# Threshold attention and SoLU: weights converted in 8 rounds, first slots turned by TensorE, slots in the order of token tiles

## The chip, the cores and the metric

The kernel runs on one core of one Trainium2 chip. The metric is the device time in microseconds of one execution. Times of runs are given with the number of runs; times of single instructions come from one profiled execution.

## What is computed

```
scores = (q @ k.T) / 8                       # batch 8, heads 8, sequence 576, head 64
thresh = max(scores, axis=-1) - tau
scores = where(scores >= thresh, scores, -1e9)
attn   = softmax(scores);   y = attn @ v     # -> x: 4608 tokens x 512
h      = x @ w_in                            # 512 x 1024
solu   = h * softmax(h)
ln     = (solu - mean) / sqrt(var + 1e-6) * g_ln
out    = ln @ w_out                          # 1024 x 512
```

All of q, k, v are 32-bit floats. `w_in` and `w_out` come as 64-bit floats[...]: the kernel reads them as integers and builds 32-bit floats from exponent, mantissa and sign.

## The kernel before

The work is cut into 144 *slots* (the list `slots`, L361), 18 for each batch: a slot is 128 queries against the 576 keys of two heads (a pair of heads, `hp`). Kind 0 and 1 are the first and second 256 queries, each in two slots (`r`) for each pair; kind 2 is the last 64 queries. Two slots of one key make a *unit*.

The schedule is written out by hand: the loop at L735 goes round by round, and round `rnd` issues, engine by engine and in this order, what is due. The main items for slot `rnd` are:

- PE: `scores` (L370), preceded by the turning of later q and k blocks (`turn`, L258) into spare columns of the same PSUM tile;
- DVE: `maxes` (L402), a maximum with its negation; ACT: `ramp` (L417, the threshold) and `exps` (L424), with `keeps` that copy turned blocks to SBUF;
- one round later POOL: `normalise` (L432: sum, power -1, two products of 128x576) and DVE: `blocks` (L442: two 32x32 transposes into `T`; after a unit's second slot, four DMAs on SP make `wT` of `T`);
- three rounds after a unit's second slot PE: `attend` (L465, 36 matmuls), and ACT: `attended` (L492).

A token tile (128 tokens) is ready for the feed-forward part (FFN) when the attention of all four pairs of its queries is done. One FFN step at most goes into a round: `h` in two quarters (`ff_h`, L520), then, some rounds later, `o` in two quarters (`ff_o`, L635). Between them DVE, ACT and POOL make the maximum, exponential, norm and the transposition. `preps` (L688) and `load_at` (L699) give the rounds in which later batches' q, k, v are turned and loaded. SP issues nearly all DMAs, in program order.

Tile pools give one buffer for each of the PSUM tags `s0` and `s1` (scores) and `p0` and `p1` (everything else, handed out by `take`, L100): whoever takes a tag waits until its last reader is done.

The weights come in 16 pieces of 128x512 (`piece`, L189): 8 of `w_in`, 8 of `w_out`. Piece x is converted in round x: `weight_a` (L208) cuts out exponent (DVE, then ACT) and mantissa (DVE); `weight_b` (L227) has three DVE operations (low word, sign, product); `weight_d` (L247) makes two SBUF-to-SBUF DMAs for a piece of `w_out`. Loads are three pieces ahead (`weight_load`, L200).

The first batch's q and k are turned by `whole_pair` (L349), which takes both PSUM tags; pairs 1, 2, 3 in rounds 0, 2, 4 (L723), after that round's exponentials.

Of the kernel before, what the change touches and what calls it, by code (L numbers as in the profile page):

```python
# [20 lines left out]
def kernel(  # L21
# [118 lines left out]
    def load_v(b, hf):  # L140
# [3 lines left out]

        d["v"] = loads.tile([P, 4, NK, D], F32, tag="v", bufs=3, name="v")
        rest = v[b, hs, 0:SM, :].rearrange("h (p t) d -> p h (t d)", t=4)
        for to, rows, of in (
            (0, slice(0, P), slice(0, P)), (4, ROWS[0], ROWS[1]), (4, ROWS[1], ROWS[0])
        ):
            nc.sync.dma_start(  # L150
                out=d["v"][rows, :, to : to + 4].rearrange("p h t d -> p h (t d)"), in_=rest[of]
            )
        for rows in ROWS:
            nc.sync.dma_start(
                out=d["v"][rows, :, NK - 1], in_=v[b, hs, SM:S, :].rearrange("h p d -> p h d")
            )
# [41 lines left out]
    raws = {}  # L198

    def weight_load(x):  # L200
        raw = work.tile(
            [P, 512], I64 if wide else F32, tag=("xh2", "xh3", "uT")[x % 3], bufs=1, name="raw"
        )
        queue = nc.scalar if x < 3 else nc.sync
        queue.dma_start(out=raw, in_=piece(x)[0])
        raws[x] = dict(raw=raw)

    def weight_a(x):  # L208
        if not wide:
            return  # L210
        d = raws[x]
        hi = d["raw"].bitcast(I32).rearrange("p (n two) -> p n two", two=2)[:, :, 1]
        d["em"] = e, m = [
            work.tile([P, 512], I32, tag=t, bufs=n, name="em") for t, n in (("ob", 2), ("xe", 1))
        ]
# [4 lines left out]

        nc.scalar.activation(out=e, in_=e, func=AF.Relu, bias=lim, scale=8388608.0)
# [4 lines left out]

    def weight_b(x):  # L227
        d = raws.pop(x)
        _, dst, unit = piece(x)
        if not wide:  # L230
            nc.vector.tensor_scalar(out=dst, in0=d["raw"], scalar1=unit, scalar2=None, op0=ALU.mult)
            return
        words = d["raw"].bitcast(I32).rearrange("p (n two) -> p n two", two=2)
        lo, hi = words[:, :, 0], words[:, :, 1]
        e, m = d["em"]
# [3 lines left out]
        nc.vector.scalar_tensor_tensor(  # L239
            out=e, in0=hi, scalar=-(2**31), in1=e, op0=ALU.bitwise_and, op1=ALU.bitwise_or  # L240
        )
        nc.vector.scalar_tensor_tensor(
            out=dst, in0=dst, scalar=unit, in1=e.bitcast(F32), op0=ALU.mult, op1=ALU.mult
        )


    def weight_d(x):  # L247
        c = x - 2 * NP
# [58 lines left out]

    def k_parts(i):
# [3 lines left out]
    def k_item(i, ts=slice(0, 4)):  # L312
# [8 lines left out]
        def keep(spare, x, r):  # L321
            (nc.vector.tensor_copy if r and not spare.get("eased") else nc.scalar.copy)(
# [6 lines left out]
    def e_item(i):  # L329
# [6 lines left out]
        def keep(spare, x, r):  # L336
# [4 lines left out]
            else:  # L341
                (nc.scalar.copy if spare.get("eased") else nc.vector.tensor_copy)(
                    out=last, in_=seen(spare, 1, x, 1)[:, 0].rearrange("p (k c) -> p c k", c=2)
                )
# [15 lines left out]

    slots = []  # L361
    for b in range(B):
# [3 lines left out]
        slots += [(b, 2, 0, 0), (b, 2, 0, 1)]  # L366

    live = {}

    def scores(s, items):  # L370
# [10 lines left out]
        for ks in (slice(SM, S), slice(0, SM)):  # L381
            for h in range(2):
                for y in range(2):
                    if kind < 2:
                        d = pairs[b * NP + hp]
                        t = P * (2 * kind + r) + 64 * y
                        lhsT = d["qT"][ROWS[h], t : t + 64]
                    else:
                        d = pairs[b * NP + r + 2 * y]
                        lhsT = d["qe"][ROWS[h]]  # L390
                    nc.tensor.matmul(  # L391
                        out=ps[h][ROWS[y], ks], lhsT=lhsT, rhs=d["kT"][ROWS[h], ks],
# [31 lines left out]
    def exps(s):  # L424
        d = live[s]
        d["sm"] = sm = small.tile([P, 2], F32, tag="sm", name="sm")
        for x, w in enumerate(d["w"]):
            nc.scalar.activation(  # L428
# [13 lines left out]
    def blocks(s):  # L442
        b, kind, hp, r = slots[s]
        key = (b, kind, hp)
# [19 lines left out]

    def attend(key):  # L465
        b, kind, hp = key
# [6 lines left out]
        for e in range(2) if kind == 2 else [None]:  # L473
            for m in range(NK):
                for u in range(2):
                    d, h0 = source(b * NP + (hp if e is None else e + 2 * u))
# [15 lines left out]
    def attended(key):  # L492
        b, kind, hp = key
# [8 lines left out]
        else:  # L502
            if hp == 0:
# [3 lines left out]
            to = xh[b, kind][:, hp].rearrange("p (r u y) -> p u r y", r=2, u=2)  # L507
# [168 lines left out]
    PER = NS // B  # L676
# [3 lines left out]
    for s, (b, kind, hp, r) in enumerate(slots):  # L680
        if r == 1:
            pv_due.append((s + LAG_PV + (s < 4), (b, kind, hp)))

    def first_slot(i):
        return PER * (i // NP) + 2 * (i % NP)

# [13 lines left out]
    for b in range(1, B):  # L700
        r = PER * (b - 1)

        for at, job, hf in zip(
            (2, 8, 9) if b > 1 else (8, 12, 15), (load_qk, load_qk, load_v), (0, 1, 0)
# [4 lines left out]
    with tc.manual_schedule():  # L709
        load_qk(0, 0)  # L710
        nc.scalar.dma_start(out=tau_t, in_=tau.partition_broadcast(P))
        constants()
        for x in range(3):
            weight_load(x)
        load_qk(0, 1)
        load_v(0, 0)
        nc.sync.dma_start(out=g_rows, in_=g_ln.rearrange("(c p) -> c p", p=P))
        whole_pair(0)
# [3 lines left out]
        pieces = {r: x for x, r in enumerate(range(16))}  # L722
        whole = {0: 1, 2: 2, 4: 3}  # L723
        load_at[3] = [lambda: load_v(0, 1)]
# [10 lines left out]
        while True:  # L735
# [29 lines left out]
            if more:  # L765
# [7 lines left out]
                scores(rnd, items)  # L773
                maxes(rnd)
                ramp(rnd, 0)
                keeps(rnd, 0)
                keeps(rnd, 1)
                ramp(rnd, 1)
                exps(rnd)
            if rnd in whole:  # L780
                whole_pair(whole[rnd])
            if rnd - 1 in live:
                normalise(rnd - 1)
# [106 lines left out]
```

## Time and profile before

| | |
|---|---|
| runs (3), us | 923.97, 929.83, 930.18; median 929.83 |
| profiled execution, us | 926.31 (span 924.5) |
| granted PE clock, mean | 0.968 |
| PE busy | 854.7 us (92%) |
| PE weight loads | 624.7 us (68%) |
| DVE busy | 679.0 us (73%) |
| ACT busy | 592.0 us (64%) |
| POOL busy | 452.8 us (49%) |
| DMA | 154.6 MB, mean 167 GB/s |
| first maximum (L408) of slots 0, 10, 20, 79, us | 14.8, 69.6, 140.2, 476.1 |

How to read it: the page cuts the span into 40 equal slices of 23.1 us and gives each engine's busy share of a slice in tenths. [...]PE's busy time says that it had work, not that it was at its peak; the length of a step is better read from the starts of successive steps in the timeline. A 32-bit matmul shows as two records. Idle time of an engine that doesn't set the end costs nothing.

### The profile page before, as it was taken

What the parts mean: (1) busy time and instruction counts of PE and PEld (TensorE: products, weight loads), DVE (VectorE), ACT (ScalarE), POOL (GpSimd) and SP (SyncE); (2) the same over time, 40 slices, a digit from 0 to 9 for tenths busy, and PEclk for the clock granted to TensorE, in tenths of its full rate; (3) what the DMA queues carried; (4) which work ended last, traced back from release to release, by engine and by line L of the source; (5) the groups of instructions that cost most, each with busy time, mean ns of one, the idle gap of its engine ahead of it and who ended that gap; (6) DMA issues with size and microseconds to landing.
All of it is one profiled execution on the core that took longest, in us unless ns stands there. A gap on an engine that the chain in (4) does not pass through costs nothing. (4 is left out here: it accounts for less than half of the span.)

```text
span 924.5 us, 39657 instructions
## 1 busy us (share of the span) xinstructions
PE 854.7 (92%) x17089; PEld 624.7 (68%) x17089; DVE 679.0 (73%) x1306; ACT 592.0 (64%) x1240; POOL 452.8 (49%) x870
## 2 busy tenths in 40 slices
PE   4657779989999999989997999999999999999997
PEld 2435457868778778867785667866677777676555
DVE  4998967768867877767876777767877777877352
ACT  4766656767767766767766676757766676776121
POOL 1554545536555555555554555545555455655120
PEclk9788799999999999999999999999999999999999
DMA  8899858985879567965889467965889565766322
GB/s 244 200 260 261 186 124 198 229 179 124 187 169 224 128 140 185 237 150 134 184 183 209 94 136 182 229 150 130 186 185 224 121 131 128 191 145 140 90 47 47
DMA packets 95470, 154.61 MB, mean 167 GB/s; under 512 B 27192, under 2 KB 69184, under 8 KB 95296
## 3 DMA queue, kind: packets, MB, share of 16 engines
q1 hardware_dynamic: 93920, 150.12, 70.3%
q8 instruction: 134, 2.20, 1.1%
q10 hardware_dynamic: 1376, 1.97, 0.6%
q14 instruction: 40, 0.33, 0.1%
HBM read 46.14 MB, written 9.44 MB: 60 GB/s over the span
## 5 line engine op out<-in xcount | busy, mean ns | idle before, releaser
L408 DVE CUSTOM_DVE_ANT_0 w<-s_ps,tau_t 128x576 f32<-128x576 f32 x288 | 206.6, 755 | 157.2 <-PE s_ps L391 133.8
L419 ACT ACTIVATE w<-s_ps,nth 128x576 f32<-128x576 f32 x288 | 207.6, 744 | 127.1 <-DVE nth L408 106.2
L642 PE MATMUL o_ps<-w,uT 64*64 64x256 f32 x4608 | 271.2, 380 | 11.3 <-DVE uT L630 9.0
L642 PEld LDWEIGHTS o_ps<-w,uT 64*64 64x64 f32 x4608 | 221.6, 134 | 70.6 <-issue 27.9
L438 POOL TENSOR_SCALAR w<-w,sm 128x576 f32<-128x576 f32 x288 | 218.6, 771 | 14.3
L428 ACT ACTIVATE w<-w,ntau 128x576 f32<-128x576 f32 x288 | 220.3, 772 | 0.0
L540 PE MATMUL h_ps<-w,xh 64*64 64x512 f32 x1856 | 218.0, 591 | 0.7 <-issue 0.7
L450 DVE STREAM_TRANSPOSE T<-w 128x576 f32<-128x576 f32 x288 | 205.8, 751 | 4.5 <-POOL w L438 4.2
L486 PEld LDWEIGHTS pv<-wT,v 64*64 64x64 f32 x5760 | 168.0, 137 | 44.1 <-issue 24.7
L391 PE MATMUL s_ps<-kT,qT 64*64 64x64 f32 (+1 forms) x2048 | 173.2, 425 | 22.5 <-ACT w L419 19.0
L486 PE MATMUL pv<-wT,v 64*64 64x128 f32 (+1 forms) x5760 | 171.2, 265 | 10.8 <-DMA wT<-T 8.3
L540 PEld LDWEIGHTS h_ps<-w,xh 64*64 64x64 f32 x1856 | 110.1, 134 | 93.3 <-issue 67.9
L435 POOL TENSOR_SCALAR sm<-sm 128x2 f32<-128x2 f32 x144 | 36.1, 251 | 275.7 <-ACT w L428 272.9
L436 POOL TENSOR_TENSOR sm<-sm,mone 128x2 f32<-128x2 f32 x144 | 107.2, 745 | 12.0
L391 PEld LDWEIGHTS s_ps<-kT,qT 64*64 64x64 f32 x2048 | 64.1, 139 | 34.9 <-ACT w L419 24.9
L604 ACT ACTIVATE V<-u,nb,rs 128x1024 f32<-128x1024 f32 x36 | 44.7, 1241 | 53.2 <-POOL nb L594 53.2
L508 ACT COPY xh<-pv 128x256 f32<-128x256 f32 x64 | 23.9, 374 | 68.1 <-PE pv L486 68.1
L630 DVE STREAM_TRANSPOSE uT<-V 128x1024 f32<-128x1024 f32 x36 | 44.1, 1224 | 23.9 <-DMA V<-u 23.9
L562 ACT ACTIVATE u<-h_ps,hm 128x1024 f32<-128x1024 f32 x36 | 40.3, 1118 | 26.4 <-DVE hm L553 20.8
L428 ACT ACTIVATION_READ_ACCUMULATOR w<-w,ntau 128x1 f32 x288 | 57.0, 198 | 0.0
L553 DVE TENSOR_REDUCE hm<-h_ps 128x1 f32<-128x1024 f32 x36 | 43.0, 1195 | 9.4 <-PE h_ps L530 6.0
L568 DVE TENSOR_TENSOR u<-h_ps,u 128x1024 f32<-128x1024 f32 x36 | 42.8, 1189 | 9.6 <-ACT u L562 9.6
(74 smaller groups left out, 609.9 us busy)
## 6 DMA issues: line engine op xcount, KB each, us to landing
wT<-T SPq DMA_DIRECT2D x288, 288.0 KB, 5.7
V<-u SPq DMA_DIRECT2D x144, 64.0 KB, 3.8
out_dram<-ob SPq DMA_DIRECT2D x72, 128.0 KB, 2.8
v<-in_v_dram SPq DMA_DIRECT2D x16, 512.0 KB, 8.3
v<-in_v_dram SPq DMA_DIRECT2D x32, 256.0 KB, 7.6
q<-in_q_dram SPq DMA_DIRECT2D x15, 512.0 KB, 6.1
k<-in_k_dram SPq DMA_DIRECT2D x15, 512.0 KB, 7.2
raw<-in_moe_w_out_dram SPq DMA_DIRECT2D x8, 512.0 KB, 9.2
```

Of the source, the lines that this page charges most:

```text
L391: nc.tensor.matmul(out=ps[h][ROWS[y], ks], lhsT=lhsT, rhs=d["kT"][ROWS[h], ks], start=True, stop=True,)
L408: nc.vector.tensor_tensor_reduce(out=w, in0=ps[:, 0:S], in1=tau_t.to_broadcast([P, S]), scale=1.0, scalar=BIG, op0=ALU.add, op1=ALU.min, a ...
L419: nc.scalar.activation(out=d["w"][x], in_=d["ps"][x][:, 0:S], func=AF.Prelu, bias=d["nth"][x], scale=-1.0, alpha=1.0e30,)
L428: nc.scalar.activation(out=w, in_=w, func=AF.Exp, bias=ntau, scale=1.0, accum_out=sm[:, x : x + 1])
L436: nc.gpsimd.tensor_tensor(out=sm, in0=sm, in1=mone, op=ALU.pow)
L438: nc.gpsimd.tensor_scalar(out=w, in0=w, scalar1=sm[:, x : x + 1], scalar2=1.0, op0=ALU.mult, op1=ALU.mult)
L450: nc.vector.transpose(out=T[:, :, r, h, :], in_=w)
L486: nc.tensor.matmul(out=to, lhsT=d["v"][ROWS[u], h0 + h, m ^ 4 * u if m < 8 else m], rhs=rhs, start=m == 0, stop=m == NK - 1,)
L540: mm = nc.tensor.matmul(out=h[ROWS[y], f], lhsT=x[ROWS[r], c, ROWS[y]], rhs=w1_parts[ROWS[r], c, part ^ r], start=part == 0 and c == 0, st ...
L604: nc.scalar.activation(out=V, in_=u, func=AF.Identity, bias=nb, scale=rs)
L630: nc.vector.transpose(out=uT, in_=d["V"].rearrange("p y (m x) -> p m y x", x=32))
L642: nc.tensor.matmul(out=d["o"][ROWS[z], 512 * r : 512 * r + 256], lhsT=d["uT"][ROWS[r], m].rearrange("p y x -> p (y x)"), rhs=w2[ROWS[r], m ...
```

## The change

- **Weights, two pieces a round in rounds 0 to 7.** `weight_a` takes over the low word's operation (3 on DVE), `weight_b` is ACT's one operation, `weight_c` the sign (DVE), and the product moves to POOL, in two operations (`weight_d`). Loads are five pieces ahead, in other buffers; the first two are issued on ACT's queue before the constants.
- **Slots 0 to 7 turned by PE.** No products, no transposes and no DMAs `wT<-T` for them: POOL makes a diagonal matrix of each head's reciprocal sums (`weigh`), PE multiplies each 128x128 block of the exponentials by it (`early_turn`, 10 matmuls a slot), which turns and normalises at once; DVE and, after round 3, ACT copy the result to SBUF; PE attends one slot at a time (`early_attend`, 10 matmuls), two rounds after the slot. The turned blocks and results use the spare columns of the score tiles and a `p` tag. The first batch's keys are kept in plain order for it (`k_plain`), and POOL copies them to the usual order (`k_spread`).
- **Order of slots.** For kind 0 and 1 of batches 0 and 1 the four pairs of one `r` come first, then those of the other: a token tile is complete after 4 slots instead of 8. A unit of these is two pairs of one `r`, attended in two halves (72 matmuls of 64 columns for 36 of 128).
- **Order of the rest.** `whole_pair` in rounds 0, 1, 2, before the exponentials; the second halves of v's first loads in rounds 6 and 7; batch 1's q, k, v loads at 8, 11, 14 (before: 8, 12, 15); in the first 36 rounds an `attend` may share a round with an `o` step.

The core of the diff:

```diff
+    RAWS = ("xh2", "xh3", "uT", "u", "xh1")
...
+    def scratch():
+        ahead["two"] = two = work.tile([P, 2, DFF // 2], F32, tag="V", bufs=1, name="two")
+        ahead["kT"] = work.tile([P, NP, S], F32, tag="T", name="kT")
+        ahead["ends"] = two[:, 0].rearrange("p (h d) -> p h d", h=H)
+        nc.gpsimd.memset(two[:, 0], 0.0)
+    def load_ends():
+        for e in range(2):
+            nc.sync.dma_start(
...
     def weight_a(x):
...
         nc.vector.tensor_scalar(
             out=e, in0=hi, scalar1=20, scalar2=0x7FF,
             op0=ALU.logical_shift_right, op1=ALU.bitwise_and,
         )
...
         nc.vector.tensor_scalar(
             out=m, in0=hi, scalar1=0xFFFFF, scalar2=0x100000,
             op0=ALU.bitwise_and, op1=ALU.bitwise_or,
         )
...
         nc.vector.scalar_tensor_tensor(
             out=dst, in0=lo.bitcast(U32), scalar=2.0**-32, in1=m, op0=ALU.mult, op1=ALU.add
         )
-        nc.vector.scalar_tensor_tensor(
-            out=e, in0=hi, scalar=-(2**31), in1=e, op0=ALU.bitwise_and, op1=ALU.bitwise_or
-        )
-        nc.vector.scalar_tensor_tensor(
-            out=dst, in0=dst, scalar=unit, in1=e.bitcast(F32), op0=ALU.mult, op1=ALU.mult
-        )
+    def weight_b(x):
+        if wide:
+            e = raws[x]["e"]
+            nc.scalar.activation(out=e, in_=e, func=AF.Relu, bias=lim, scale=8388608.0)
+    def weight_c(x):
+        if wide:
+            e = raws[x]["e"]
+            nc.vector.scalar_tensor_tensor(
+                out=e, in0=words(x)[1], scalar=-(2**31), in1=e,
+                op0=ALU.bitwise_and, op1=ALU.bitwise_or,
+            )
+        if x + len(RAWS) < NW:
+            weight_load(x + len(RAWS), nc.sync)
     def weight_d(x):
...
+            nc.gpsimd.tensor_scalar(
+                out=dst, in0=dst, scalar1=unit, scalar2=1.0, op0=ALU.mult, op1=ALU.mult
+            )
+            nc.gpsimd.tensor_tensor(out=dst, in0=dst, in1=d["e"].bitcast(F32), op=ALU.mult)
...
+    def k_spread(i):
+        of = k_plain(i)
+        to = k_parts(i)
+        first = of[:, 0:SM].rearrange("p (t r k c) -> p r c t k", t=4, r=2, c=2)
+        for r in range(2):
+            nc.gpsimd.tensor_copy(
+                out=to[:, 4 * r : 4 * r + 4].rearrange("p t c k -> p c t k"), in_=first[:, r]
+            )
+        nc.gpsimd.tensor_copy(
+            out=to[:, NK - 1], in_=of[:, SM:S].rearrange("p (k c) -> p c k", c=2)
+        )
...
+    EARLY = 2 * NP
+    OUTER = {(0, 0), (0, 1), (1, 0), (1, 1)}
+    for b, kind in OUTER:
+        o = PER * b + EARLY * kind
+        slots[o : o + EARLY] = [(b, kind, hp, r) for r in range(2) for hp in range(NP)]
...
+    def weigh(s):
+        d = live[s]
+        sm = d["sm"]
+        nc.gpsimd.tensor_scalar(out=sm, in0=sm, scalar1=1e-9, scalar2=None, op0=ALU.add)
+        nc.gpsimd.tensor_tensor(out=sm, in0=sm, in1=mone, op=ALU.pow)
+        d["diag"] = diag = work.tile([P, 2, P], F32, tag="ob", name="diag")
+        for h in range(2):
+            nc.gpsimd.tensor_scalar(
+                out=diag[:, h], in0=ident, scalar1=sm[:, h : h + 1], scalar2=1.0,
+                op0=ALU.mult, op1=ALU.mult,
+            )
+    def early_turn(s, rnd):
+        d = live.pop(s)
+        tag, tp = take("tw")
+        last = live[rnd]["ps"][1][:, S : S + P]
+        for h in range(2):
+            w = d["w"][h]
+            for t in range(5):
+                if t < 4:
+                    o = 512 * h + P * t
+                    to, of = tp[:, o : o + P], w[:, P * t : P * t + P]
+                else:
+                    to, of = last[ROWS[h]], w[:, SM:S]
+                nc.tensor.matmul(out=to, lhsT=of, rhs=d["diag"][:, h], start=True, stop=True)
...
+        on_act = rnd > 3
+        nc.vector.tensor_copy(out=wT[:, 0:4], in_=tp[:, 0:512].rearrange("p (t k) -> p t k", t=4))
+        (nc.scalar.copy if on_act else nc.vector.tensor_copy)(
+            out=wT[:, 4:8], in_=tp[:, 512:1024].rearrange("p (t k) -> p t k", t=4)
+        )
+        (nc.scalar.copy if on_act else nc.vector.tensor_copy)(out=wT[:, 8], in_=last)
+        pairs_free.append(tag)
+    def early_attend(s, rnd):
+        b, kind, hp, r = slots[s]
+        wT = early.pop(s)
+        y = live[rnd]["ps"][0][:, S : S + P]
+        d, h0 = source(hp)
+        for t in range(5):
+            for h in range(2):
+                of = d["v"][:, h0 + h, t] if t < 4 else ahead["ends"][:, 2 * hp + h]
+                nc.tensor.matmul(
+                    out=y[ROWS[h]], lhsT=of, rhs=wT[:, 4 * h + t if t < 4 else 8],
+                    start=t == 0, stop=t == 4,
+                )
...
@@ the loop
+                if rnd - 2 in early:
+                    early_attend(rnd - 2, rnd)
                 maxes(rnd)
+                if rnd < EARLY:
+                    weight_b(2 * rnd)
                 ramp(rnd, 0)
                 keeps(rnd, 0)
                 keeps(rnd, 1)
                 ramp(rnd, 1)
+                early_attended()
+                if rnd < EARLY:
+                    weight_c(2 * rnd)
+                    weight_a(2 * rnd + 1)
+                if rnd in whole:
+                    whole_pair(whole[rnd])
                 exps(rnd)
-            if rnd in whole:
-                whole_pair(whole[rnd])
             if rnd - 1 in live:
-                normalise(rnd - 1)
+                (weigh if rnd - 1 < EARLY else normalise)(rnd - 1)
+            if 0 <= rnd - 1 < EARLY:
+                early_turn(rnd - 1, rnd)
+            if rnd < NP:
+                k_spread(rnd)
...
-            if rnd in pieces:
-                x = pieces[rnd]
-                weight_b(x)
-                if x + 3 < len(pieces):
-                    weight_load(x + 3)
-                if x + 1 < len(pieces):
-                    weight_a(x + 1)
-            if rnd - 1 in pieces:
-                weight_d(pieces[rnd - 1])
-                w2_done = pieces[rnd - 1] == NW - 1
+            if rnd < EARLY:
+                if rnd:
+                    weight_d(2 * rnd - 1)
+                weight_c(2 * rnd + 1)
+                if 2 * rnd + 2 < NW:
+                    weight_a(2 * rnd + 2)
+                weight_d(2 * rnd)
+            elif rnd == EARLY:
+                weight_d(NW - 1)
+                w2_done = True
```

Between the two exponentials of a slot before 8, `exps` also issues `weight_b(2 * s + 1)`.

## The prediction

> **What bounds it now.** I read the page's slices first, then busy time by stretch, then the order of instructions engine by engine, then the timeline of the start. A *round* r is one slot: it runs from the first maximum (L408) of slot r to that of slot r+1.
>
> ```profile
> PE   4657779989999999989997999999999999999997
> DVE  4998967768867877767876777767877777877352
> PEclk9788799999999999999999999999999999999999
> ```
> PE is the bound, except in the first six or seven slices (some 150 us), where DVE is full and PE is not. The stretches say how much:
> ```profile
> core 0: us, PE busy (x) PEld busy (x) DVE busy (x) ACT busy (x) POOL busy (x), PEclk, DMA share, GB/s
> 20.00:40.00 20.00, 11.81 (x209) 7.20 (x209) 19.34 (x41) 16.44 (x37) 10.83 (x15) 0.76 0.71 177
> 60.00:80.00 20.00, 12.69 (x242) 9.74 (x242) 16.08 (x34) 11.27 (x24) 9.45 (x13) 0.76 1.06 270
> 300.00:320.00 20.00, 20.00 (x422) 16.37 (x418) 16.92 (x34) 15.86 (x34) 9.78 (x21) 1.00 0.55 123
> ```
> From 20 to 40 us DVE works 19.3 of 20 us and PE 11.8, at 0.76 of its clock. At 300 us PE works 20.0 of 20.
> PE's timeline where it is full gives the price of a step, start to start:
> ```profile
> 147.16 3.70 PE L540 MATMUL h_ps<-w,xh 64*64 64x512 f32 x32
> 150.59 1.24 PE L391 MATMUL s_ps<-kT,qT 64*64 64x64 f32 x16
> 151.56 3.72 PE L642 MATMUL o_ps<-w,uT 64*64 64x256 f32 x64
> ```
> An `h` step is 3.43, scores about 0.95, an `o` step 3.45 (155.02 to 151.56, the next row); likewise `pv` is 1.96 (164.44 to 166.40), 2.1 when cut in halves, a group of 20 turns 0.6. Rounds summed from these agree with their measured length within 0.2 us wherever PE is full, so I use them for both kernels.
> The last view is POOL beside DVE in the start:
> ```profile
> 62.58 0.75 DVE L242 SCALAR_TENSOR_TENSOR w<-w,gs,em 128x512 f32<-128x512 f32 x1
> 63.25 0.42 DVE L216 TENSOR_SCALAR em<-raw 128x512 int32<-128x512 int32 x1
> 63.58 0.42 DVE L222 TENSOR_SCALAR em<-raw 128x512 int32<-128x512 int32 x1
> ...
> 62.76 1.28 POOL L436 TENSOR_TENSOR sm<-sm,mone 128x2 f32<-128x2 f32 x1
> ...
> 303.77 0.71 POOL L436 TENSOR_TENSOR sm<-sm,mone 128x2 f32<-128x2 f32 x1
> ```
> The same two-element power takes 0.71 us alone and 1.28 beside a weight conversion, ending 0.04 us after DVE's L222 does: POOL is held while DVE converts.
>
> [...] The full-width row (L530) shows 190 ns a load, hidden under 452 ns a matmul (21.7/48).
>
> **Part 1: where the work goes.** The order of PE's instructions has five more FFN steps done by round 20 (12 against 7). But the lead shrinks: steps need attention's results, at most one goes in a round, and the new kernel comes to rounds with none (14, 23, 24, 37, 46, 56, 65, 74). From round 79 both orders are the same, to the last instruction. So the tail isn't shorter; the change is worth what it saves of PE's idle time before round 79, which starts at 476.1 us now. Two stretches follow.
>
> **Part 2: rounds 0 to 9.** Before: 14.8 to 69.6 us, about 5.5 us a round, DVE's sum: maxima 1.35, transposes 1.43, conversion 0.34+0.33+0.60+0.72+0.61=2.6.
> After, per round until 7: DVE 2 conversions of (0.34+0.33+0.60+0.70)=3.94, maxima 1.35, transposes gone; PSUM copies of `wT` instead, 0.62 for 512 columns (by the slope of the `kT` copies, 216 ns at 64 and 416 at 256), 0.22 for 128: all three on DVE in rounds 1 to 3 (6.75 us a round), one from round 4 (5.9). POOL: the two 771 ns products go; it gets two diagonals (0.5), and per weight a scaling (735x512/576=0.65)[...], the sums and powers 1.1, `k_spread` 0.8 in rounds 0 to 3. ACT: 4.5, keeps 1.53 in 0 to 2, copies 0.74 from 4. PE: 10 turning matmuls, 20 records. Unshown; from L530 a quarter of 452, so 20x0.113=2.3 us with loads hidden, 20x(0.113+0.19)=6.1 with none; I take 2.3/0.76=3.0. Early attention 10 matmuls, 1.1 to 2.3; I take 1.4.
> Chains, from the program's waits. In rounds 1 and 2 the turning matmul waits for `whole_pair`'s keeps (same PSUM tag), and the next scores for the third copy (same PSUM tile): first ramp 0.8 after the maximum, two ramps 1.4, keeps 1.5, turning 3.0, copies left 0.85, conversion 2.0: 9.6, in round 2 10.2 with early attention ahead. Round 0, without turning: 7.2. Rounds 3 to 5: DVE's and POOL's conversion work one after the other is 3.94+5.3=9.2 (9.7 in round 3 with parts of it idle-covered); without contention the chain over ACT's copies is 6.3. I take 8.5, 7.8, 7.8. Rounds 6 and 7 hold `h` behind turning: 0.3+1.4+3.0+3.44+0.75=8.9; in 7 also the FFN maximum 1.2 and a conversion step ahead of the next maximum: 10.0. Round 8 6.3 (ACT's chain), round 9 4.5. Sum 80.8. The first maximum stands behind the first conversion, which waits for its weights (L216 at 14.1); they are issued 1.8 us earlier (2.9 against 4.7): start about 13.8. Round 10 is then at 94.6, against 69.6.
> Behind these waits: on PE, the next scores stand behind the turning matmul, and DVE's maxima wait for those; on POOL, `weigh` stands behind two products, and the turning matmul waits for it; on ACT, from round 4 the copies stand behind both exponentials.
> DMAs: 16 `wT<-T` transfers go (4 units, 288 KB each); the weights' 8.4 MB come in 8 longer rounds, below the 246 GB/s that 40 to 60 us shows. Five buffers give a load two rounds (over 14 us) against 9.2 us to landing: nothing, but 1 us of DVE per us late if a load takes longer. On SP, batch 1's q and k (round 8) now queue behind `w2` swaps that wait for POOL; due at round 10, 10.8 us later, landing 6 to 7: nothing, with little to spare; each us later would be a us of round 10.
> Edits at nothing: the second halves of v go from the start to rounds 6 and 7, first used by `pv` in round 13; the two loads of v's ends (POOL zeroes their tile first) are due in round 2, over 15 us after issue; plain keys change the keeps' target only, not their count; the loads at 11 and 14 for 12 and 15 follow the pairs' earlier first slots. Rounds of more than 6 us hide each; bare, each is one landing, 6 to 8 us.
>
> **Part 3: rounds 10 to 78.** PE's work after: 69x0.91 scores + 30x3.44 `h` + 30x3.43 `o` + 17x1.95 + 16x2.10 `pv` + 596x0.03 turns = 353.8. (Before: 360.5, in 406.5 us.) Loss: in before, rounds 20 to 78 lose 19.2 us; 7.1 of it in three rounds with no FFN step (28, 29, 38: 7.6, 4.6 and 4.5 us between their L408 in DVE's timeline, 5.6 on average, for 3.3, 3.5 and 2.9 of PE's work), 0.22 a round elsewhere. After: 61x0.22=13.2, and eight such rounds 8x5.6-25.0=19.6. Sum 386.6. Round 79 then starts at 481.2, 5.1 later than now.
> The profiled execution takes 926.3, so 931.4; on the median 929.8, 934.9. The profiled one lies inside the three runs; I say **934**.
>
> **Rivals.** A chance for each; 1% (9.3 us) is about what a measurement of this kernel can tell from no change.
> *As summed*, 0.42: extra early work eats the saving; -4 to +10, so 926 to 940.
> *Turning matmuls with bare weight loads*, 0.27, slower: a full-width load (190 ns) isn't covered by a 113 ns matmul. At 6.1 instead of 3.0, +3.1 in rounds 1, 2, 6, 7, about 1 in 3: +13.4, 947. It decides from 4.0 us a slot. For it: loads twice as wide as any in the start[...]; against: L530's loads do hide.
> *POOL becomes the bound of rounds 1 to 7*, 0.15: its product takes 2.0 instead of 1.2 held by DVE: 1.6 more in five rounds, +8, 942. For it: the held power; against: POOL is idle half of the time now.
> *The saving stays*, 0.16: rounds without FFN work cost no more than PE's other rounds, the loss falls from 33 to 13 us: 914, and 919 with a little of it. For it: rounds 29 and 38 took 4.5; against: 28 took 7.6.
> *The tail gets shorter by the five steps (17 us)*: excluded by the order from round 79 on.
>
> **The numbers.** Faster 0.15 (the fourth case). Slower: 0.27+0.10 of the third+0.04 of the first=0.41. The rest, 0.44, within 1%. Range 917 to 952: the fourth case's upper part up to the second's, with its clock some 5 us worse.
>
> **What would show it.** Round 10's first maximum near 95 us (before: 69.6); round 79's near 481; turning records of about 150 ns start to start (300 would be the second case); POOL's products over 1.2 us and stretched beside conversions; eight rounds of over 5 us without FFN work. Wrong if round 10 comes before 85 us, or if rounds 10 to 78 take under 370 or over 400.

## The result, and the profile after

The changed kernel takes 987.37 us (median of 4 runs, 985.72 to 1003.04) against 926.9 of the kernel before beside it: 1.0651 times as long, with an interval of 1.0577 to 1.0725. The run of 1003.04 was in a slower state and has no part in the ratio. The profiled execution takes 988.3 (span 986.5). The forecast of 934, with a range up to 952, was wrong by 53 us; "slower" had 0.41.

The slices of the page after, to be laid beside those of before:

```profile
PE   4777878958999989999898999999999999999997
DVE  5774655644677866877686787777777777887442
PEclk9888989978999999999999999999999999999999
```
DVE is no longer full in the first slices (7, 7, 4, 6 in slices 2 to 5 for 9, 9, 8, 9), yet PE isn't either; PE has a 5 in slice 9 (197 to 222 us), and between slices 10 and 22 four digits of 8. The same stretches as before:

```profile
core 0: us, PE busy (x) PEld busy (x) DVE busy (x) ACT busy (x) POOL busy (x), PEclk, DMA share, GB/s
20.00:40.00 20.00, 12.79 (x148) 9.94 (x148) 13.71 (x22) 11.13 (x28) 13.24 (x22) 0.77 0.49 163
60.00:80.00 20.00, 14.69 (x112) 9.48 (x116) 13.48 (x28) 10.36 (x22) 9.15 (x12) 0.83 0.50 129
300.00:320.00 20.00, 17.57 (x494) 12.82 (x489) 13.93 (x27) 12.45 (x29) 9.33 (x19) 1.00 0.79 197
```
From 20 to 40 us DVE works 13.7 of 20 us where it worked 19.3, POOL more (13.2 for 10.8), and no engine is full: a chain of waits from engine to engine sets the rounds. At 300 us PE works 17.6 of 20 at a full clock, although nothing of the new start is left there.

The first maxima (L408 before, L486 after) give the time by stage:

| us | before | predicted | after | after less predicted |
|---|---|---|---|---|
| first maximum | 14.8 | 13.8 | 11.6 | -2.2 |
| rounds 0 to 9 | 54.8 | 80.8 | 101.5 | +20.7 |
| rounds 10 to 78 | 406.5 | 386.6 | 435.1 | +48.5 |
| round 79 to the end of the span | 448.4 | 448.4 | 438.3 | -10.1 |

The differences sum to 56.9, which is 988.3 less the 931.4 that was forecast for the profiled execution.

**Rounds 0 to 9.** Three things stand in the timeline. First POOL's product beside DVE (start, duration, engine and line; the bracket is the idle time before an instruction and what ended it):

```profile
29.81 1.32 POOL L286 TENSOR_TENSOR w<-w,w 128x512 f32<-128x512 f32 x1 [0.69 <-DVE w L271]
29.92 1.49 DVE L253 TENSOR_SCALAR w<-raw 128x512 int32<-128x512 int32 x1
```
L253 takes 0.42 us alone. The product starts when DVE's L271 ends, and here it meets L253, which waits it out: 29.81+1.32 is 31.13, and 29.92+1.49 is 31.41, less than 0.3 us later. It happens to 8 of the 16 pieces, twice in rounds 1 and 2 and once in rounds 0, 3, 4 and 5, and each time L253 takes 1.07 us more.

Second, PE's clock. In rounds 3, 4 and 5 the trace grants half the clock from 51.2 to 54.6, from 61.4 to 64.8 and from 71.6 to 75.0. In these stretches lie the scores and the early attention, for which the next maximum waits. Round 4 of the changed kernel, and after it round 4 of e7 (a run below), where the same rows have the full clock:

```profile
61.22 2.06 PE L469 MATMUL s_ps<-kT,qT 64*64 64x64 f32 x12 [1.62 <-ACT wT L578]
63.21 1.85 PE L589 MATMUL s_ps<-wT,v 128*64 128x128 f32 x16
```
```profile
60.48 1.19 PE L468 MATMUL s_ps<-kT,qT 64*64 64x64 f32 x12 [0.94 <-ACT wT L577]
61.60 1.09 PE L588 MATMUL s_ps<-wT,v 128*64 128x128 f32 x16
```
From the start of these twelve score records to the next maximum it is 4.1 us in each of rounds 3, 4 and 5, and 2.5 at the full clock (rounds 3 to 5 of e3, 4 and 5 of e7): 1.6 us a round.

Third, round 7, from 85.5 to 101.2:

```profile
79.58 3.66 PE L687 MATMUL h_ps<-w,xh 64*64 64x512 f32 x32
83.34 0.10 POOL L106 MEMSET mark<- 128x1 f32 x1 [10.50 <-PE h_ps L687]
...
86.20 1.26 POOL L286 TENSOR_TENSOR w<-w 128x512 f32<-128x512 f32 x1
...
89.03 1.06 POOL L551 TENSOR_SCALAR diag<-ident,sm 128x128 f32<-128x128 f32 x2
89.80 2.08 PE L569 MATMUL tw<-diag,w 128*128 128x128 f32 x8 [4.34 <-POOL diag L551]
```
POOL's queue holds a marker (L106, `fence`, called by `ff_h`) that waits for the first `h` step. POOL stands 10.5 us before it; the conversions of round 6 and the diagonals of round 7 stand behind it, and PE waits 4.3 us for those.

**Rounds 10 to 78.** PE's timeline shows attention in halves stopping in its middle:

```profile
131.47 1.80 PE L629 MATMUL pv<-wT,v 64*64 64x64 f32 x108
136.48 1.23 PE L629 MATMUL pv<-wT,v 64*64 64x64 f32 x34 [3.22 <-issue]
...
140.37 0.51 PE L629 MATMUL pv<-wT,v 64*64 64x64 f32 x18
143.48 2.83 PE L629 MATMUL pv<-wT,v 64*64 64x64 f32 x96 [2.60 <-issue]
...
218.47 0.48 PE L629 MATMUL pv<-wT,v 64*64 64x64 f32 x4 [7.04 <-DMA v<-in_v_dram]
```
"issue" means that PE waited for nothing the profile shows. Between round 10's and round 79's first maximum there are 15 such gaps of 0.9 us or more, 31.3 us in all; before there was one, of 1.3. The last line is another matter, in round 24: v of batch 1's second half is issued at 212.1, in the same round that wants it. The queues of the page name what the gaps have to do with, the row of instructions that are fetched:

```profile
q8 instruction: 141, 2.31, 1.1%
```
Before, the row has 134 packets. In the trace each is 16,384 bytes and takes 1.2 us on average; one lands 1.3 to 1.8 us before the end of 13 of the 14 gaps up to 540 us (the gap that ends at 136.48 follows one that landed at 135.16). The other ends at 220.28, while the parts of the late v are still landing (218.3 to 221.0).

### The profile page after: what moved, and what is told of

Same layout as the page of the kernel before. It is cut to its first block, busy times and chain, and to the rows that moved or that the text cites. A ratio compares the mean times of both kernels' runs of the same rounds, so it can differ in the third digit from the quotient of the medians.

```text
span 986.5 us, 41486 instructions
## 1 busy us (share of the span) xinstructions
PE 892.9 (91%) x17985; PEld 660.9 (67%) x17985; DVE 676.0 (69%) x1286; ACT 595.4 (60%) x1256; POOL 475.9 (48%) x915
## 5 line engine op out<-in xcount | busy, mean ns | idle before, releaser
L486 DVE CUSTOM_DVE_ANT_0 w<-s_ps,tau_t 128x576 f32<-128x576 f32 x288 | 206.8, 755 | 214.4 <-PE s_ps L469 150.4
L789 PEld LDWEIGHTS o_ps<-w,uT 64*64 64x64 f32 x4608 | 230.7, 133 | 56.1 <-issue 20.7
L687 PE MATMUL h_ps<-w,xh 64*64 64x512 f32 x1856 | 223.2, 601 | 2.5 <-issue 2.4
L518 POOL TENSOR_SCALAR w<-w,sm 128x576 f32<-128x576 f32 x272 | 204.9, 766 | 13.5
L529 DVE STREAM_TRANSPOSE T<-w 128x576 f32<-128x576 f32 x272 | 194.7, 752 | 5.4 <-POOL w L518 5.4
L629 PEld LDWEIGHTS pv<-wT,v 64*64 64x64 f32 x6336 | 162.2, 138 | 51.2 <-issue 44.2
L469 PE MATMUL s_ps<-kT,qT 64*64 64x512 f32 (+1 forms) x2048 | 177.4, 424 | 20.4 <-issue 6.3
L629 PE MATMUL pv<-wT,v 64*64 64x128 f32 (+1 forms) x6336 | 164.3, 251 | 23.5 <-issue 16.1
L515 POOL TENSOR_SCALAR sm<-sm 128x2 f32<-128x2 f32 x136 | 30.7, 226 | 253.1 <-ACT w L508 250.0
L516 POOL TENSOR_TENSOR sm<-sm,mone 128x2 f32<-128x2 f32 x136 | 96.7, 711 | 11.3
L700 DVE TENSOR_REDUCE hm<-h_ps 128x1 f32<-128x1024 f32 x36 | 43.2, 1199 | 15.7 <-PE h_ps L687 10.2
L709 ACT ACTIVATE u<-h_ps,hm 128x1024 f32<-128x1024 f32 x36 | 40.3, 1119 | 21.9 <-DVE hm L700 15.7
```

Source lines behind the costliest of these rows:

```text
L469: nc.tensor.matmul(out=ps[h][ROWS[y], ks], lhsT=lhsT, rhs=kT[ROWS[h], ks], start=True, stop=True,)
L486: nc.vector.tensor_tensor_reduce(out=w, in0=ps[:, 0:S], in1=tau_t.to_broadcast([P, S]), scale=1.0, scalar=BIG, op0=ALU.add, op1=ALU.min, a ...
L516: nc.gpsimd.tensor_tensor(out=sm, in0=sm, in1=mone, op=ALU.pow)
L518: nc.gpsimd.tensor_scalar(out=w, in0=w, scalar1=sm[:, x : x + 1], scalar2=1.0, op0=ALU.mult, op1=ALU.mult)
L529: nc.vector.transpose(out=T[:, :, r, h, :], in_=w)
L629: nc.tensor.matmul(out=to, lhsT=d["v"][ROWS[u], h0 + h, m ^ 4 * u if m < 8 else m], rhs=rhs, start=m == 0, stop=m == NK - 1,)
```

## The experiments

Medians are of four runs, ratios against runs of before beside them. *Round 10 at*, *rounds 10 to 78* and *gaps* (0.9 us or more, no releaser, from 60 us to round 79's first maximum) are of its one profiled execution, which lies up to 10 us from the median (e12 9.7 and e7 8.6 below, e4 8.1 above); *fetches* are the page's packets of that row.

| kernel | median us | ratio to before | round 10 at | rounds 10 to 78 | gaps | fetches |
|---|---|---|---|---|---|---|
| before | 923.5 to 926.9 | | 69.6 | 406.5 | 1.3 | 134 |
| changed | 987.4 | 1.058 to 1.073 | 113.1 | 435.1 | 31.3 | 141 |
| e1, v earlier | 976.3 | 1.051 to 1.065 | 110.9 | 425.0 | 21.6 | 141 |
| e2, old order | 958.8 | 1.024 to 1.044 | 114.5 | 400.6 | 10.2 | 134 |
| e3, swap | 977.9 | 1.051 to 1.066 | 107.2 | 424.2 | 23.9 | 141 |
| e4, before, all in halves | 1016.3 | 1.095 to 1.110 | 72.7 | 455.1 | 42.5 | 170 |
| e5, no turning | 936.1 | 1.009 to 1.017 | 88.8 | 403.7 | 3.1 | 134 |
| e6, turning twice | 988.9 | 1.066 to 1.081 | 117.7 | 425.5 | 18.4 | 142 |
| e7, product on DVE | 979.4 | 1.052 to 1.064 | 103.7 | 420.6 | 25.2 | 141 |
| e8, e2 with e3 | 952.9 | 1.024 to 1.036 | 108.5 | 399.5 | 8.7 | 134 |
| e9, e5 with e7 | 940.2 | 1.008 to 1.020 | 89.2 | 402.0 | 1.1 | 134 |
| e10, e2, e3, e7 | 950.7 | 1.021 to 1.034 | 106.9 | 395.3 | 8.6 | 135 |
| e11, first h later | 967.4 | 1.037 to 1.050 | 109.5 | 408.9 | 13.2 | 141 |
| e12, before, order alone | 946.9 | 1.013 to 1.027 | 68.7 | 423.0 | 15.4 | 141 |
| e13, before, h in quarters | 946.4 | 1.016 to 1.030 | 69.7 | 419.2 | 12.3 | 150 |
| e14, turning first | 990.5 | 1.067 to 1.079 | 114.1 | 428.1 | 26.8 | 141 |

The theory from this trace: the start is long by POOL's product and its waits, the rest by the new order, through PE's instructions and the late v. The rivals: PE's turning sets the start; the order costs nothing by itself.

**The order.**

```diff
 e1, v earlier (changed kernel)
-        load_at.setdefault(r + PER + 6, []).append(lambda b=b: load_v(b, 1))
+        load_at.setdefault(r + PER + (6 if b > 1 else 3), []).append(lambda b=b: load_v(b, 1))
 e2, old order (changed kernel)
-    OUTER = {(0, 0), (0, 1), (1, 0), (1, 1)}
+    OUTER = {(0, 0)}
 e4, before, all in halves (the same columns, twice the matmuls)
-        for e in range(2) if kind == 2 else [None]:
+        for e in range(2):
```


> The changed kernel with the second half of batch 1's v loaded in round 21 instead of 24. Theory (late load): the new slot order needs it in round 24, so round 24 (18.95 us, 7 of them PE waiting for v) falls to 5 to 7 us and the whole is 10 to 14 us shorter, 974 to 977 against 987. Rival (the transfers only change places: SP's queue or the DMA engines are what is late): round 24 gets shorter but the loss turns up within a few rounds, and the whole moves by less than 4 us.

> The changed kernel with the old slot order except in the first eight slots (weights in 8 rounds and turning by PE stay; no units in two halves; batch 1's v is then needed two rounds later). Theory (instruction supply): PE's gaps that wait for nothing shown, 31 us in rounds 10 to 78, come from the doubled instruction count of the halved units and from bunched rounds; they fall below 8 us and with the late v the whole is 35 to 45 us shorter, 942 to 952. Rival (the gaps come from the transfers of the start, shifted by the longer first rounds): the gaps stay above 20 us, only the late v is saved: 970 to 978.

> The kernel before with every unit's attention cut into two halves of 64 columns: the same work in twice as many matmuls and weight loads, everything else as before. Theory (instruction supply): a halved unit costs 0.15 us of PE and on average 1 to 1.5 us of gaps that wait for nothing shown: 64 units, 70 to 100 us more, about 1000 to 1025. Rival (halves cost what their steps show where PE is full): 64 x 0.15 = 10 us more, 933 to 940.

e1: 11 us shorter; round 24 falls from 18.95 to 5.28 us, but round 22 grows from 7.55 to 13.91 by a new gap of 4.1 us and other waits. e2: 28.6 us shorter, less than the theory's 35, with gaps of 10.2 us for under 8, and rounds 10 to 78 at 400.6. e4: 93 us longer, as the theory has it, with one edit that adds no column of work. The group of its attention and its row of fetches:

```profile
L486 PE MATMUL pv<-wT,v 64*64 64x64 f32 x10368 | 190.9, 224 | 39.8 <-issue 34.8 <-DMA wT<-T 3.2 <-ACT qe L338 1.8
```
```profile
q8 instruction: 170, 2.79, 1.2%
```
Before, the group's idle time had 0.6 us of "issue". PE has 21697 matmul records for 17089, 4608 more, and as many weight loads: 9216 instructions, which is 36 packets (170 less 134) of 256. So by this count the packets hold PE's instructions, 256 in each; twice 17089 by 256 is 133.5, the 134 packets of before. All 19 gaps before round 79 end 1.2 to 1.9 us after one landed. Spread over the 36 fetches, the 93 us are 2.6 us each.

e12 puts the order alone into the kernel before (`OUTER = {(0, 1), (1, 0), (1, 1)}`, the split units, the loads at 8, 11, 14, an `attend` beside an `o` step in the first 36 rounds; weights and first eight slots untouched), and e13 doubles another kind of instruction there:

```diff
 e13, before, h in quarters (loop over c, then n in 0, 1)
-                f = slice(512 * (part ^ r), 512 * (part ^ r) + 512)
+                f = slice(512 * (part ^ r) + 256 * n, 512 * (part ^ r) + 256 * n + 256)
```


> The kernel before with the slot order alone, for the last eight slots of batch 0 and the sixteen of batch 1, with their attention in halves and the loads moved as in the change; weights and first eight slots untouched. If the order costs by itself (PE's instruction supply in rounds with attention in halves, and v of batch 1's second half late in round 24), rounds 10 to 78 take 425 to 440 us against 406.5, gaps without a releaser 20 us and more against 1.3, and the whole is 940 to 955. If it costs only together with the changed start, the whole is within 1% of before.

> The kernel before with each h matmul cut into two of 256 columns: 1152 more matmuls and as many weight loads, the same columns in all. If PE's gaps in the slot order come from instructions wanted faster than they arrive (attention in halves: 288 matmuls and loads in some 2.1 us), the longer h step with 64 in 3.4 us asks for far less than arrives and the whole stays within 1% of before, gaps without a releaser under 6 us before 540 us. If the number of PE's instructions counts whatever their rate, 2304 more cost half of what 4608 more cost in the run with all attention in halves: about 46 us, so 970.

e12: 23 us longer, with 15.4 us of gaps and 3.3 of waiting for v: the order costs by itself; rounds 10 to 78 took 423.0, just short of the 425 expected, and the gaps fell short of their 20. That an `attend` may share a round with an `o` step isn't what costs: e2 keeps it. e13 fell between its two cases. It is 20.5 us longer and not within 1%, so the rate isn't everything; but its 16 more fetches (2048 records and as many loads; the expectation's 1152 are program matmuls of all tiles, and a matmul is two records, 32 for an `h` step's 16) cost 1.3 us each, half of what they cost in e4. Both seem to count: the number of instructions, and how densely they come (e4's attention asks for 288 in some 2.1 us, e13's `h` for 128 records and loads in 3.4, not the 64 of the expectation). e13's gaps end like the others, 8 of 8 up to 540 us, 1.3 to 1.7 us after a fetch.

**The start.**

```diff
 e3, swap (at both places where the pair stands)
-                    weight_c(2 * rnd)
                     weight_a(2 * rnd + 1)
+                    weight_c(2 * rnd)
 e7, product on DVE
-            nc.gpsimd.tensor_scalar(
-                out=dst, in0=dst, scalar1=unit, scalar2=1.0, op0=ALU.mult, op1=ALU.mult
-            )
-            nc.gpsimd.tensor_tensor(out=dst, in0=dst, in1=d["e"].bitcast(F32), op=ALU.mult)
+            nc.vector.scalar_tensor_tensor(
+                out=dst, in0=dst, scalar=unit, in1=d["e"].bitcast(F32), op0=ALU.mult, op1=ALU.mult
+            )
 e6, turning twice
+                for _ in range(2):
                     nc.tensor.matmul(out=to, lhsT=of, rhs=d["diag"][:, h], start=True, stop=True)
 e11, first h later
-            ready.append((rnd + 1, [(0, 0, r)]))
+            ready.append((rnd + 3, [(0, 0, r)]))
```


> The changed kernel with each weight's sign operation moved behind the next weight's three first operations, so that POOL's product, which waits for the sign, starts beside PSUM copies or maxima instead of beside DVE's mantissa operation (1.48 us instead of 0.42 beside it). Theory[...]: 1.06 us saved for each of some 12 pieces, less where the round waits for something else: round 10 starts 7 to 13 us earlier than 113.1, the whole is 6 to 13 us shorter. Rival (the chain of turning, copies and scores sets rounds 1 to 7, and DVE's held operation is covered): round 10 moves by less than 3 us.

> The changed kernel with each turning matmul issued twice into the same place (the second overwrites the first with the same values). It doubles what PE does for turning and nothing else. If PE's turning stands on the path of rounds 1, 2, 6 and 7 and partly of the others, round 10 comes 15 to 28 us later than the 113.1 of the changed kernel. If conversions on DVE and POOL set the rounds and the turning runs beside them, it comes less than 6 us later.

> The changed kernel with the last product of each weight back on DVE as one instruction (0.72 us, as before), POOL's scaling and product gone. If POOL's product beside DVE's instructions is what stretches the rounds (held 1.06 us a piece, and the diagonals late behind the products), DVE's mantissa instruction falls back from 1.48 to about 0.4 us and round 10 comes 5 to 12 us earlier than 113.1. If DVE is full in any case, 16 x 0.72 = 11.5 us of added work make it come as late or up to 10 us later.

> The changed kernel with the first two token tiles released to the FFN two rounds later, so that the first h step goes in round 8 instead of 6. In the changed kernel POOL stands idle 10.5 us at a marker that waits for that h step, which stands behind round 6's turning; four scalings and products and the diagonals of round 7 stand behind the marker. If that ring makes round 7's 15.7 us, round 7 falls to 9 to 11 us and round 10 comes 4 to 8 us earlier. If round 7 is long because of its own work, the h steps only move and round 10 comes less than 2 us earlier.

e3: round 10 comes 5.9 us earlier, a little under what was expected. Rounds 3 to 5 are 6.0 us shorter, the other rounds cancel. But the holding is not gone: in rounds 4 and 5 DVE's L249 meets the product instead (0.97 to 1.17 us for 0.42). PE has the full clock in these rounds, which is 4.9 of the 6.0 us; the scores start 0.2 to 0.6 us earlier in each. The number nearly came, by another way than expected.

e7: 9.4 us earlier. L253 is back at its own time, and rounds 3, 4, 5 take 8.61, 7.84 and 7.88 us (in the changed kernel 10.09, 10.15, 10.16):

```profile
57.08 0.42 DVE L249 TENSOR_SCALAR w<-raw 128x512 int32<-128x512 int32 x1
...
57.42 0.42 DVE L253 TENSOR_SCALAR two<-raw 128x512 int32<-128x512 int32 x1
```
Of these 6.1 us, 4.1 are PE's full clock and 2.0 the scores, which start 0.6 to 0.7 us earlier. Round 7 falls from 15.68 to 10.88, as no product stands behind the marker. Two rounds hold the two causes apart. In round 3 of e14 (below) L253 is held, 1.51 us, and scores and attention have the full clock: 8.47 us. In round 4 of e10 nothing holds L253, and they have half the clock: 10.27. What sets the clock back in these rounds isn't shown; the longest wait of PE in rounds 3 to 5 of the changed kernel is 1.62 us.

e6: twice the turning makes round 10 only 4.5 us later, but this is a sum of two effects. Rounds 1, 2, 6, 7 and 8 are 1.1 to 1.6 us longer each, so the turning does stand on their path in part. Rounds 4 and 5, with more work, are 1.2 us shorter each (8.95 for 10.15 and 10.16): PE has the full clock from 40 to 91 us. e11: round 7 falls from 15.68 to 9.95, so the wait at the marker is its cause; rounds 8 and 9 take back 2.8 with the moved `h`, and round 10 comes 3.6 earlier, a little under the 4 to 8. Its rounds 10 to 78 fall too, by 26 us, with the same 141 fetches: gaps are 18 us less and round 24 takes 9.3 us for 18.95. Its attention in halves goes into other rounds (12, 15, 16, 19 for 13, 14, 16, 18), beside other steps. The number of fetches alone thus doesn't fix the loss; what of the arrangement does isn't shown.

In e5 the first eight slots go the way of before (`OUTER = set()`, `normalise` and `blocks` for all, keys written in place, `whole_pair` in rounds 0, 2, 4); e9 is e5 with e7's product; e14 moves `early_turn` ahead of `whole_pair`; e8 and e10 are combinations.

> The changed kernel with its weights in eight rounds, but with the turning by PE, the diagonals, the plain keys and the slot order all undone: the first eight slots go the way of the kernel before (scaled on POOL, transposed on DVE, rearranged by DMA). It tells what the weights alone cost. If the conversions set rounds 0 to 7 (DVE 3.94 of conversion, 2.78 of maxima and transposes, and two pieces in which the [...]instruction is held 1.06 us by POOL's product: 8.8 a round), round 10 starts at 94 to 98 us against 113 in the changed kernel and 69.6 before, and the whole takes 938 to 948. If the turning is what makes the rounds long, rounds 0 to 7 take about 6.7 us each, round 10 starts near 78 and the whole is within 1% of before (917 to 933).

> The run without turning (weights in eight rounds, attention as before), with the last product of each weight on DVE as one instruction. DVE's own work is then 2 x 2.68 of conversion and 2.78 of maxima and transposes, 8.1 us a round against 8.6 measured with the product on POOL. If DVE's sum is what stands in these rounds, round 10 comes 1 to 4 us earlier than 88.8 and the whole is 932 to 936. If POOL held DVE for more than its own work (as the run with the product on DVE showed beside turning, 9.4 us), round 10 comes near 80 and the whole near 927.

> The changed kernel with the turning of rounds 1 and 2 issued ahead of the whole pair, whose copies from PSUM then stand on ACT behind the exponentials. In the changed kernel PE stands 5.25 and 3.27 us at the turning until those copies have left the PSUM tile. If that wait lengthens rounds 1 and 2, the two together fall from 25.9 to 20 to 23 us. If the conversions or the keys (the next scores need the pair's copies, which now end about 2 us later) hold these rounds anyway, they stay within 1.5 us.

> The changed kernel with two edits that each helped alone: only the first batch's first eight slots in the new order, and the next weight's first part ahead of the sign instruction. If the gains add (they lie in different stretches: before round 10 and after it), about 950 (945 to 954), round 10 near 108 and rounds 10 to 78 near 400. If they don't, about 959.

> The changed kernel with three edits: only the first batch's first eight slots in the new order, the next weight's first part ahead of the sign instruction, the last product on DVE. With the product on DVE the swap has less to give (nothing of POOL stands beside the mantissa instruction). If both act on the same wait, round 10 near 102 and the whole near 947; if they add, round 10 near 99 and the whole near 943.

e5: 936.1, 1.3% above before and just under the 938 to 948 expected: the weights in eight rounds, by themselves, make round 10 19 us later; 88.8 is earlier than the 94 expected, and rounds 2 to 6 take 8.2 to 8.6 us. e9 gained nothing (89.2, with a first maximum 1.2 us later): what DVE is no longer held, it works. The groups of e9's L250 (with the product on DVE) and of e5's from 10 to 90 us, in that order:

```profile
L250 DVE TENSOR_SCALAR w<-raw 128x512 int32<-128x512 int32 x8 | 3.3, 417 | 0.0
```
```profile
L250 DVE TENSOR_SCALAR w<-raw 128x512 int32<-128x512 int32 x8 | 8.1, 1015 | 0.0
```
Summed over all conversion groups DVE is busy 49.3 us in e5 and 50.2 in e9, where 12.1 are the products. Beside turning (e7) the product's way back to DVE did pay, since there the diagonals stand behind POOL's products. e14: rounds 1 and 2 take 27.9 us together, not less than the 25.9 of the changed kernel; the wait for the pair's copies goes, but then the copies come last, and the next scores wait for them, and run at half the clock (the same sixteen records take 1.2 to 1.3 us at the full one):

```profile
29.36 2.20 PE L469 MATMUL s_ps<-kT,qT 64*64 64x64 f32 x16 [1.71 <-ACT kT L405]
```
e8: the gains add (952.9 for 950 expected). e10: 950.7 and 106.9, above both of its cases: with e8's edits in, the product on DVE brought 1.6 us in round 10 (half of it ahead of the first maximum) and nothing beyond the interval in all. No run is below before; e5, with the weights alone, comes nearest.

## Why the prediction was wrong

The parts add up along e5 and e2: weights +12 us (936.1), turning of the first slots with what it needs +23 (958.8), the order of the other slots +29 (987.4). The forecast had +5 for all.

*Right.* The lead of five steps is given back before round 79, and the tail has no part in a gain by it; its 10 us less are for the same order, and 4.6 of them are three gaps of before (5.85 us) against one of after (1.27). Before also has 6.8 us at half the clock there, after none until its end; the rest isn't settled. The turning records start 112 ns apart at the full clock, where a load's own record takes 192: so their loads are hidden, as the 113 of the sum had it. At half the clock they start 214 apart, with 333 for a load. A product of POOL takes 1.26 to 1.32 us, twice 1.58 (over the 1.2 forecast, an estimate that no row of before showed; "stretched" was right for POOL's neighbour rather than for POOL). The first maximum comes earlier, by 3.2 us where 1.0 was forecast. Six of the eight rounds with no FFN step take 4.5 to 6.2 us, for 5.6 forecast.

*Wrong, the largest: "so I use them for both kernels", said of the steps' lengths, and with it "16x2.10 `pv`".* 2.10 us for attention in halves was read where it stood alone among long steps, and the sum for rounds 10 to 78 has no term for instructions. The prediction's own sign of being wrong, over 400 us for these rounds, came: 435.1. Twelve units that are newly in halves, in rounds 13 to 38, bring 1728 records and loads (seven fetches), and the gaps are 31.3 us where the stage is 48.5 over the forecast. e4 and e12 show that attention in halves brings such gaps into the kernel before; e2, without it, still has 10.2 us of them, so not all of the 31.3 is the order's. "Loss" was taken from before for rounds with no FFN step, at 5.6 us; of these, round 14 took 8.2 and round 24 18.95. The sum itself, done again, is 386.7 for 386.6.

*Wrong: "Edits at nothing", and in it "the loads at 11 and 14 for 12 and 15 follow the pairs' earlier first slots".* The last of these loads, v's second half of batch 1, stayed in round 24, while the order brought its first use there: 7.0 us of waiting, shown by e1. The remaining 10 us of this stage are not put down to one cause. A part is the clock: PE is busy for 33.9 us at half the clock in this stage and for 18.9 in before's, which costs at most half of the difference, 7.5 us (an estimate; the twelve score records took 1.7 times as long with the half, 2.06 us for 1.19).

*Mis-sized: rounds 3 to 5, "8.5, 7.8, 7.8".* Measured 10.1 each. The forecast took numbers between two sums, 6.3 us without contention and 9.2 with DVE and POOL one after the other, and put its 0.76 of the clock on the turning alone. What it left out is PE's half clock for the scores and the early attention, 1.6 us a round; L253 behind POOL's product delays the scores by 0.6 to 0.7 more. That e7 and e3 come near the forecast (7.84 and 8.32 in round 4) is luck: their chains are others than the one that was summed. As to the holding: the trace of before had shown a power on POOL at 1.28 us beside DVE's conversions and 0.71 alone, and the third rival then priced a POOL product of 2.0 us, the author's estimate. The holding went the other way here: the products beside L253 took 1.30 to 1.32 us, L253 1.48 to 1.50 for 0.42.

*Wrong: round 7, "10.0".* Measured 15.7. "Rounds 6 and 7 hold `h` behind turning" saw PE's queue; not that POOL's queue has a marker that waits for the same `h`, and behind it the diagonals of the next turning. Without that wait it takes 9.95 (e11), though PE has half the clock there in part. Rounds 6 and 8 are together 2.7 us over their forecast, for a reason that stays open.

*Mis-sized, not settled: rounds 1 and 2, 9.6 and 10.2 forecast, 12.9 and 13.0 measured.* In round 1 the turning takes 4.9 us in place of 3.0 (22.98 to 27.89; eight records take 2.05 us, where round 2's first eight take 1.13): the trace has half the clock from 20.4 to 27.3. What set it back isn't shown. The last conversion takes 3.2 us for 2.0. In round 2 PE works from 36.02 to the next maximum at 45.1 with one wait, of 0.55, and the trace has half the clock from 37.5 to 44.3: the turning's second head takes 2.60 us and its first 1.43, the scores' last twelve records 2.18 (1.19 in round 1), the attention 1.85 (1.31). But doubling the turning costs 1.5 us a round (e6), putting it first gains none (e14, where the half clock falls on the scores and on the attention, which takes 2.40 us for 1.31), and the product on DVE gains none there (e7): several chains are nearly as long, and which of them ends last when one is cut was not found out. Over all, the half clock is about 9 of the 20.7 us by which rounds 0 to 9 exceed the forecast (1.9, 2.5 and 3 x 1.6 in rounds 1 to 5), an estimate from these rows.

*Wrong: the rivals.* "Turning matmuls with bare weight loads" was to decide from 4.0 us a slot; a slot takes PE 3.1 us or, at half the clock, 4.9, with the loads hidden in both (starts of 112 and 214 ns for loads of 192 and 333). Twice the matmuls lengthen its rounds 1, 2, 6 and 7 by 1.3 to 1.6 us each (e6), about half of the 3.1 at which it was priced. None of the rivals had the slot order lose by itself.

## What to carry to other kernels

Count an engine's instructions as well as their columns: where a change cuts the same columns into more and smaller matmuls, cost it also by fetches (an added one came with 2.6 us in e4, 1.3 in e13), and not by its length among longer steps. Work moved to another engine can cost the first engine too, as POOL's product did L253 (1.49 us for 0.42); write down which instructions meet. For every engine's queue, list the markers in it that wait for others, and who stands behind them (POOL's first took 10.5 us here). Where a chain runs through PE, ask for each of its steps, and not for one, at what clock it will run (2.06 us or 1.19 for the same twelve records).

## What the runs showed of the hardware

- A packet of the instruction row is 16,384 bytes in before and in the changed kernel, and by count holds 256 of PE's instructions (36 more packets for 9216 more matmul and load records in e4). Of the 44 gaps of 0.9 us or more without a releaser, from 60 to 540 us, in before, changed, e4 and e13, 43 end 1.2 to 1.9 us after one landed; such stretches make up 10 to 12% of that time. Most fetches have no gap: in before 63 land between round 10 and round 79, and there is one gap. An edit's added time over its added fetches was 2.6 us in attention cut in halves and 1.3 in `h` cut in quarters. That PE runs out of instructions is the reading that fits all of this; no record says it directly.
- DVE's L253 (128x512) took 1.48 to 1.50 us in the 8 places of the changed kernel where it started 0.1 us behind POOL's product L286, and ended 0.3 us after the product each time; elsewhere it took 0.41 to 0.52.
- More work on PE made two rounds shorter: with the turning doubled, rounds 4 and 5 take 8.95 us for 10.15, as the trace then grants PE the full clock there and not the half (e6). The same twelve score records take 1.19 us at the full clock and 2.06 with the half.
- The same order of instructions on PE from round 79 on took 448 us in before's profiled execution and 438 in the changed kernel's.
